# A Fourier sequence transform as seven block products in two passes, and where its coefficient sums are made

## The chip, the cores and the metric

The kernel runs on one core of one Trainium2 chip. The metric is the device time of one execution in microseconds; three runs of the kernel before are given below. The engines are TensorE (PE in the profile, its weight loads PEld), VectorE (DVE), ScalarE (ACT), GpSimd (POOL) and SyncE (SP), which issues almost all transfers of this kernel, in order.

## The reference

Four layers follow each other on x of 2048 rows and 512 columns: a Fourier mixing layer, an attention layer with a compressive memory, and both once more. Each is added to its input, which is normalised row by row first. The change concerns the Fourier layers:

```python
a = jnp.einsum("bsd,ed->bse", x, dft_hid_re)
b = jnp.einsum("bsd,ed->bse", x, dft_hid_im)
y = jnp.einsum("ts,bse->bte", dft_seq_re, a) - jnp.einsum("ts,bse->bte", dft_seq_im, b)
```

The kernel takes the sequence transform first: it multiplies the normalised rows by the real and by the imaginary sequence matrix (2048 x 2048 each), and then each result by its hidden matrix (512 x 512), summing both.

## The kernel before, in words

**Precision.** A float32 operand is used as two parts: `split` (lines 95 to 105) writes hi with a ScalarE copy (L99) and lo with a subtraction on VectorE (L101). `matmul3` (L107) makes three matmuls of them: hi by hi, hi by lo, lo by hi, each 128 x 128 by 128 x 512.

**Tiles.** The output of the sequence transform is made in four column groups (`tcn`, 0 to 3) of 512 sequence positions. The sum runs over the 2048 rows: 8 steps `k` of 128 rows in each half (`HALF` = 8), so rows `k` and `k + 8` belong together. The normalised rows are the 16 tiles `xa` (tag "w", 16 buffers), split into hi and lo. The coefficients of one `tcn` and `k` are four blocks of 128 x 512: re0, re1 (real, lower and upper half of the rows) and im0, im1.

**First transform** (`direct`). `contract` (L306) makes, for each column group, the real and the imaginary product whole: 8 k x 2 halves x 2 parts x 4 pieces of 128 columns x 3 = 384 matmuls into eight PSUM banks (tile u). `read_pairs` (L272) loads the four blocks in two transfers of 512 KB into raw buffers ("craw" for even k, half of a ring for odd k), splits them, and then forms four sums for the second transform (L296): re0+im0, im0+im1, re0+im0+im1 and re0+im0+im1+re1. They lie in the other half of the ring, one buffer of four blocks, and are stored in DRAM (`sums`, L299), 1 MiB for each `tcn` and `k`. At the end of a group ScalarE (L328) and VectorE (L330) move the eight banks to the tiles `c`.

**Second transform.** Seven products of blocks, P1 to P7, take the place of eight: per group 7 x 8 k x 2 halves x 3 = 336 matmuls (tile m, `product`, L333). Their right sides are blocks of coefficients or the stored sums; the left sides are columns of `xa`, or of `xb` and `xs`, differences and sums of rows that `add_rows` (L218) makes. For P1 and P7 the second half of the lower rows' columns has been replaced by a difference (in `normalise`, L208). `PHASES` (L52) gives the order: P1 and P7 for groups 0 and 1, P2 and P4 for these, the same for 2 and 3, then P6, P5 and P3 for all four. `read_block` (L256) loads one block for one product, 256 KB, into one of eight places of a ring (`cring`) and splits it (512 wide). `TERMS` (L43) says how a product enters the tiles `c`; VectorE adds it from PSUM (L356).

**After each sequence transform** `split_u` and `hidden` (L359 on) make the product with the hidden matrices (tile y), and the attention follows.

**Order of the work.** The kernel is written as generators, each placed on a hand-written line of slots with `place(order, generator, slots)`; a slot of the transforms is about six matmuls for one product. The program order that results is a priority: a scheduler orders each engine's instructions by it, TensorE keeps it strictly. Every `yield` is the end of one slot's part. `read_pairs` stands 12 slots ahead of its matmuls with its loads and 4 ahead with its splits; `read_block` 10 and 4 ahead. The right sides live in the tags "chi" and "clo" with three buffers each. `load_rows` (L121) uses four buffers "xt". `a1`, `b1`, `a2`, `b2` (L1002 to L1005) are the first slots of the four layers.

## Time and profile before

| | |
|---|---|
| runs of the kernel before | 1906.6, 1908.78, 1909.02 us (median 1908.78) |
| the profiled execution | 1911.1 us from its first to its last instruction (this span is the time that the profile gives for it) |
| mean granted TensorE clock | 0.985 |
| ScalarE busy | 1062.9 us, 56% |
| transfers | 296.49 MB, mean 155 GB/s |
| read from HBM, written to HBM | 192.95 MB, 100.66 MB |

How to read it: a table by stages gives, for each stretch of the span, the busy time of every engine with its number of instructions, then the granted clock (PEclk, 1.00 is full speed), the busy share of the 16 DMA engines and what they moved in GB/s. A row of the timeline gives the start, the duration, the engine, the line, the operation, out<-in and the shape; what stands in brackets is the engine's idle time before it and what ended it. A row of waits gives the sum, the number and the longest. Durations of matmuls overlap each other.

### The profile page before, as it was taken

The numbers are of one execution on the slowest core, as the hardware profiler recorded it, in microseconds if no ns is written. First come the engines' busy times: TensorE is split into PE (matmuls) and PEld (weight loads), VectorE is DVE, ScalarE is ACT, GpSimd is POOL, SyncE is SP. The second block draws the span as 40 slices with busy tenths as digits, with TensorE's granted clock in tenths as the row PEclk, the third lists the DMA queues.
The fourth block names the chain that finished last, engine by engine and source line by source line (L and its number), as shares of the span: only waits on it lengthen the run. The fifth ranks groups of instructions, "written<-read, shape, count | busy, mean of one in ns | idle before, by whom it ended". The sixth has DMA issues, their size and how long they took to land. (4 is left out here: it accounts for less than half of the span.)

```text
span 1911.1 us, 31877 instructions
## 1 busy us (share of the span) xinstructions
PE 1809.7 (95%) x10336; PEld 1301.0 (68%) x10336; DVE 1311.1 (69%) x4073; ACT 1062.9 (56%) x2292; POOL 512.5 (27%) x831
## 2 busy tenths in 40 slices
PE   7899999999899999999889999999988999999998
PEld 6678888888556656665458888787865655666654
DVE  8654545462787787777866687777558778777773
ACT  3221213331578777767664465453337877777775
POOL 4200000002345344446431000000124443434432
PEclk9999999999899999999999999999999999999998
DMA  6665555353544333434445787563444434444231
GB/s 224 233 208 199 189 191 198 115 173 121 178 125 148 118 120 115 149 119 134 134 154 181 222 251 225 164 204 127 159 150 139 144 108 134 126 133 142 91 117 45
DMA packets 165655, 296.49 MB, mean 155 GB/s; under 512 B 17776, under 2 KB 66928, under 8 KB 165488
## 3 DMA queue, kind: packets, MB, share of 16 engines
q1 hardware_dynamic: 162224, 293.68, 47.5%
q8 instruction: 81, 1.33, 0.3%
q10 hardware_dynamic: 3264, 0.79, 0.2%
q14 instruction: 86, 0.70, 0.1%
HBM read 192.95 MB, written 100.66 MB: 154 GB/s over the span
## 5 line engine op out<-in xcount | busy, mean ns | idle before, releaser
L603 DVE CUSTOM_DVE_ANT_0 junk<-nat,mask 128x512 bf16<-128x512 f32 (+3 forms) x1024 | 496.6, 485 | 203.2 <-PE nat L87 183.9
L669 ACT ACTIVATE pT<-sT 128x512 f32<-128x512 f32 x640 | 370.3, 598 | 15.0 <-ACT sT L668 2.2
L87 PE MATMUL u<-chi,xa 128*128 128x512 f32 x1024 | 321.1, 395 | 10.9 <-DVE xa L97 7.3
L672 POOL TENSOR_SCALAR_AFFINE_SELECT pT<-pT 128x256 f32<-128x256 f32 (+1 forms) x448 | 197.4, 455 | 431.5 <-ACT pT L669 366.8
L87 PE MATMUL sT<-stkq,stkk 99*128 99x256 bf16 (+3 forms) x1024 | 250.7, 307 | 17.5 <-DVE mx L603 8.8
L87 PE MATMUL nat<-stkk,stkq 96*128 96x512 bf16 (+3 forms) x1024 | 246.5, 302 | 20.8 <-DVE mx L603 12.4
L668 ACT ACTIVATE sT<-sT 128x256 f32<-128x256 f32 (+1 forms) x640 | 208.6, 334 | 63.9 <-PE sT L87 56.7
L87 PEld LDWEIGHTS u<-chi,xa 128*128 128x128 f32 x1024 | 195.4, 191 | 52.8 <-issue 7.2
L87 PE MATMUL u<-clo,xa 128*128 128x512 f32 x512 | 202.6, 396 | 9.6 <-DVE clo L101 9.6
L142 POOL TENSOR_TENSOR r<-ve,half_neg 128x2 f32<-128x2 f32 (+1 forms) x33 | 24.0, 728 | 696.5 <-DVE ve L140 692.9
L87 PE MATMUL y<-wdt,us 128*128 128x512 f32 x768 | 182.5, 391 | 1.2 <-DVE wdt L101 1.2
L87 PEld LDWEIGHTS <-stkk 99*128 99x128 bf16 x1024 | 82.6, 99 | 146.3 <-issue 127.9
L87 PEld LDWEIGHTS y<-wdt,us 128*128 128x128 f32 x768 | 143.4, 188 | 31.6 <-DVE wdt L101 2.0
L87 PE MATMUL pv_bank<-pT,vt 128*17 128x128 f32 (+3 forms) x2048 | 158.7, 440 | 1.7 <-POOL pT L672 1.6
L87 PEld LDWEIGHTS <-stkq 96*128 96x128 bf16 x1024 | 94.9, 99 | 75.9 <-issue 37.3
L87 PE MATMUL po<-wo,oh 128*128 128x512 f32 x384 | 125.7, 443 | 7.6 <-DVE oh L101 5.4
L87 PE MATMUL pvv<-wv,xT 128*128 128x512 f32 x384 | 127.0, 443 | 3.9 <-DVE mx L603 3.9
L87 PE MATMUL pqk<-xT,wq 128*128 128x512 f32 x384 | 129.9, 447 | 0.0
L87 PE MATMUL pqk<-xT,wk 128*128 128x512 f32 x384 | 127.8, 442 | 0.0
L87 PEld LDWEIGHTS u<-clo,xa 128*128 128x128 f32 x512 | 97.7, 191 | 32.5 <-DVE clo L101 12.2
L87 PEld LDWEIGHTS pv_bank<-pT,vt 128*17 128x17 f32 x2048 | 57.6, 98 | 90.7 <-issue 77.0
L99 ACT ACTIVATE clo<-cring 128x512 fp32r<-128x512 f32 x112 | 70.6, 631 | 69.1 <-DVE chi L101 37.9
(138 smaller groups left out, 3032.0 us busy)
## 6 DMA issues: line engine op xcount, KB each, us to landing
sum<-sring SPq DMA_DIRECT2D x32, 1024.0 KB
cring<-sum SPq DMA_DIRECT2D x128, 256.0 KB
stkq<-scrq SPq DMA_DIRECT2D x64, 384.0 KB
stkk<-scrk SPq DMA_DIRECT2D x64, 384.0 KB
cring<-in_ct SPq DMA_DIRECT2D x96, 256.0 KB
sring<-in_ct SPq DMA_DIRECT2D x32, 512.0 KB
xt<-mid SPq DMA_DIRECT2D x64, 256.0 KB
craw<-in_ct SPq DMA_DIRECT2D x30, 512.0 KB
```

Of the source, the lines that this page charges most:

```text
L87: return tc.keep_in_program_order(op(*args, **kwargs))
L99: A.activation(hi, src, AF.Copy, scale=scale)
L142: G.tensor_tensor(out=r, in0=ve, in1=half_neg[:, :n], op=ALU.pow)
L603: V.tensor_tensor_reduce(junk[:, :n], src, mask[:, 512 - n :], 1.0, 3e38, ALU.add, ALU.min, dst,)
L668: A.activation(blocks, blocks, AF.Relu)
L669: A.activation(dst, ps, AF.Exp, scale=-SCALE)
L672: G.affine_select(blocks, blocks, pattern=[[0, n] for n in blocks.shape[1:-1]] + [[1, P]], compare_op=ALU.is_ge, fill=0.0, base=0, channel ...
```

## The change

The first transform makes column group 0 as before. Groups 1 to 3 are made of the seven products, in two passes: P1, P2, P7 and P4 (eight PSUM banks) for each of the three groups, then P3, P5 and P6 (six banks) for each. The coefficients lie in DRAM as four blocks side by side (re1, re0, im0, im1), 8 KB per row of a partition.

- `read_direct` loads group 0 and makes no sums. Once `contract(0)` has used row tile k, `change_rows` loads its row again, normalises it and replaces the second half of `xa[k]` by the difference. `add_rows` runs during the last group of pass 1.
- `read_all` (pass 1) loads four blocks in one transfer of 1 MiB, splits P2's and P1's (1024 wide at once), makes four sums, one of them (im0+im1) on GpSimd, splits P4's and P7's, and stores two sums (512 KB).
- `read_rest` (pass 2, and the last phase of the second transform) loads the two stored sums and im1. `store_sums` makes the two sums of group 0 during pass 2.
- In the second transform `read_upper` loads three blocks and makes im0+im1 itself; `read_lower` loads one block and one stored sum, and adds them. The last phase runs in the order P3, P5, P6. Of the sums, two of four are stored.
- Raw blocks rotate over two halves of the ring, a tile "quad" (in place of "craw") and, in the first transform, the space of the attention's v tiles. In the second transform the first eight reads have the two ring halves alone.
- P6 enters one of its three terms on GpSimd, from a copy that ScalarE makes.
- The attention's tiles pT2 and praw and its v tiles lie in these shared places; the ones in the v tiles are set later. The attention and second transform start 24 slots earlier in the slot line.

```diff
-PHASES = (
-    (("P1", "P7"), (0, 1)),
-    (("P2", "P4"), (0, 1)),
-    (("P1", "P7"), (2, 3)),
-    (("P2", "P4"), (2, 3)),
-    (("P6", "P5", "P3"), range(4)),
-)
+PHASES = {
+    True: (
+        (("P1", "P2", "P7", "P4"), range(1, TC)),
+        (("P3", "P5", "P6"), range(1, TC)),
+    ),
+    False: (
+        (("P1", "P7"), (0, 1)),
+        (("P2", "P4"), (0, 1)),
+        (("P1", "P7"), (2, 3)),
+        (("P2", "P4"), (2, 3)),
+        (("P3", "P5", "P6"), range(TC)),
+    ),
+}
...
+        def raw_set():
+            if not ring:
+                ring.append(sb.tile([P, 8, 512], F32, name="cring", tag="xT", bufs=1))
+                ring.append(itertools.cycle([ring[0][:, :4], ring[0][:, 4:]]))
+                ring.append(itertools.cycle([1, 0, 0] + [2] * direct))
+            reads[0] += 1
+            if direct or 8 < reads[0]:
+                home = next(ring[2])
+                if home == 1 and reads[0] < total - 6:
+                    if len(ring) < 4:
+                        ring.append(quad("cquad"))
+                    return ring[3]
+                if home == 2:
+                    return spare[:, :4]
+            return next(ring[1])
...
+        def rights(src):
+            hi, lo = pair("chi", "chi", 3), pair("clo", "clo", 3)
+            split(hi, lo, src)
+            return [(hi[:, j], lo[:, j]) for j in range(2)]
...
+        def store_sums(tcn, k):
+            raw = raw_set()
+            nc.sync.dma_start(raw[:, 1:], ct[tcn, k, :, 1:])
+            yield
+            add(raw[:, 1], raw[:, 1], raw[:, 2])
+            add(raw[:, 3], raw[:, 1], raw[:, 3])
+            nc.sync.dma_start(sums[tcn, k], raw[:, 1::2])
+            yield
+
+        def read_all(tcn, k):
+            raw = raw_set()
+            nc.sync.dma_start(raw, ct[tcn, k])
+            yield
+            pair_sum = spare_pairs[k % 2]
+            add(pair_sum[:, 1], raw[:, 2], raw[:, 3], G)
+            right[tcn, "P2", k], right[tcn, "P1", k] = rights(raw[:, :2])
+            yield
+            add(raw[:, 2], raw[:, 1], raw[:, 2])
+            add(raw[:, 3], raw[:, 2], raw[:, 3])
+            later.append(add(pair_sum[:, 0], raw[:, 0], raw[:, 3]))
+            yield
+            right[tcn, "P4", k], right[tcn, "P7", k] = rights(pair_sum)
+            nc.sync.dma_start(sums[tcn, k], raw[:, 2:])
+            yield
+
+        def read_upper(tcn, k):
+            raw = raw_set()
+            nc.sync.dma_start(raw[:, 1:], ct[tcn, k, :, 1:])
+            yield
+            add(raw[:, 2], raw[:, 2], raw[:, 3])
+            right[tcn, "P1", k], right[tcn, "P7", k] = rights(raw[:, 1:3])
+            yield
+
+        def read_lower(tcn, k):
+            raw = raw_set()
+            nc.sync.dma_start(raw[:, 0], ct[tcn, k, :, 0])
+            nc.sync.dma_start(raw[:, 1], sums[tcn, k][:, 1])
+            yield
+            add(raw[:, 1], raw[:, 0], raw[:, 1])
+            right[tcn, "P2", k], right[tcn, "P4", k] = rights(raw[:, :2])
+            yield
+
+        def read_rest(tcn, k):
+            raw = raw_set()
+            nc.sync.dma_start(raw[:, :2], sums[tcn, k])
+            nc.sync.dma_start(raw[:, 2], ct[tcn, k, :, 3])
+            yield
+            right[tcn, "P3", k] = one_right(raw[:, 2])
+            right[tcn, "P5", k], right[tcn, "P6", k] = rights(raw[:, :2])
+            yield
...
+        def change_rows(k):
+            xt = load_rows(x_in[k])
+            yield
+            xn = normal(xt, row_mv[:, k], row_r[:, k : k + 1])
+            a, b = slice(0, D // 2), slice(D // 2, D)
+            V.tensor_tensor(out=xn[:, b], in0=xn[:, a], in1=xn[:, b], op=ALU.subtract)
+            split(xa[k][:, 0, b], xa[k][:, 1, b], xn[:, b])
             yield
...
             for m in range(2):
+                if len(TERMS[name]) > 2:
+                    copy = new_raw()
+                    A.activation(copy, ps[m], AF.Copy)
                 for j, base, op in TERMS[name]:
                     dst = c[tcn, j][:, m]
                     if base is None:
                         A.activation(dst, ps[m], AF.Copy)
+                    elif len(TERMS[name]) > 2 and j == (1, 0):
+                        G.tensor_tensor(out=dst, in0=c[tcn, base][:, m], in1=copy, op=op)
                     else:
                         V.tensor_tensor(out=dst, in0=c[tcn, base][:, m], in1=ps[m], op=op)
...
+        t = start
         if direct:
...
+            place(2, contract(0), run_from(t, 4 * HALF, 2))
+            for k in range(HALF):
+                place(3, read_direct(0, k), [t + 8 * k - 12, t + 8 * k - 4])
+                place(3, change_rows(k), [t + 8 * k + 4, t + 8 * k + 9])
+            t += 8 * HALF
+        for names, tcns in PHASES[direct]:
+            n = len(names)
+            for tcn in tcns:
+                for j, name in enumerate(names):
+                    place(2, product(tcn, name), run_from(t + j, HALF, n))
                 for k in range(HALF):
...
+                    at = {4: [-14, -7, -6, -2], 3: [-10, -5], 2: [-9, -6]}[n]
+                    place(3, readers[names](tcn, k), [t + k * n + d for d in at])
+                t += HALF * n
+        u = t - len(tcns) * 3 * HALF
+        for k in range(HALF):
+            if direct:
+                place(3, add_rows(k), [u - 25 + 4 * k, u - 24 + 4 * k])
+                place(3, store_sums(0, k), [u + 7 * k, u + 7 * k + 5])
+            else:
                 place(3, add_rows(k), [u - 48 + 6 * k, u - 44 + 6 * k])
...
-    b1 = a1 + TC * 8 * HALF + LEAD
+    b1 = a1 + (8 + 7 * (TC - 1)) * HALF + LEAD
```

More of the change, by code (lines that the diff above doesn't have):

```diff
@@ L184, in spectral_infini_kernel @@
     sums = {
-        (tcn, k): dram.tile([4, P, 512], F32, name=f"sum{tcn}_{k}") for tcn in range(TC) for k in range(HALF)
+        (tcn, k): dram.tile([P, 2, 512], F32, name=f"sum{tcn}_{k}") for tcn in range(TC) for k in range(HALF)
     }
@@ L521, in proj @@
             rem = sb.tile([P, 512], F32, name="rem", bufs=1)
[L522 removed]
+            raw = new_raw() if with_phi else rem
             sign = -1.0 if n == "q" else 1.0
```

142 lines of the change are left out of this document (66 added, 76 removed).

## The prediction

> **What bounds the kernel now.** I read the page first, then the stages of the first transform, then what TensorE waited for there, then the stages of the second transform.
>
> ```profile
> span 1911.1 us, 31877 instructions
> PE 1809.7 (95%) x10336; PEld 1301.0 (68%) x10336; DVE 1311.1 (69%) x4073; ACT 1062.9 (56%) x2292; POOL 512.5 (27%) x831
> L87 PE MATMUL u<-chi,xa 128*128 128x512 f32 x1024 | 321.1, 395 | 10.9 <-DVE xa L97 7.3
> L87 PE MATMUL u<-clo,xa 128*128 128x512 f32 x512 | 202.6, 396 | 9.6 <-DVE clo L101 9.6
> ```
>
> TensorE (PE) is busy 95% of the span. The first sequence transform is the tile u: 1024 + 512 = 1536 matmuls, 384 for each of four column groups. The duration (395 ns) overlaps the next matmul; what counts is the distance of starts. A table by stages, and two rows near the end of the transform:
>
> ```profile
> core 0: us, PE busy (x) PEld busy (x) DVE busy (x) ACT busy (x) POOL busy (x), PEclk, DMA share, GB/s
> 112.40:377.90 265.50, 265.50 (x1173) 219.84 (x1172) 134.10 (x175) 67.64 (x85) 0.00 (x0) 1.00 0.54 184
> 7.00:112.40 105.40, 91.88 (x365) 72.73 (x366) 76.33 (x147) 25.69 (x34) 32.54 (x23) 0.95 0.66 223
> ...
> 373.75 0.62 PE L87 MATMUL u<-chi,xa 128*128 128x512 f32 x2
> ...
> 377.15 0.62 PE L87 MATMUL u<-chi,xa 128*128 128x512 f32 x2
> ```
>
> Between the last two rows lie 15 matmuls in 3.40 us: 0.2267 us each. From 112.4 us on TensorE is never idle, VectorE (DVE) is half busy. All 1536 at that pace are 348.2 us; the transform took 377.9 - 7.0 = 370.9. The missing 22.7 us lie in the first group. What the engines waited for up to 150 us:
>
> ```profile
> PE u L87 <- DVE clo L101: 9.6, 6, 3.2
> PE u L87 <- ACT chi L99: 3.3, 1, 3.3
> DVE sring L296 <- DMA sum<-sring: 22.8, 5, 6.0
> ...
> 65.00:70.00 5.00, 3.51 (x17) 2.58 (x15) 5.00 (x7) 1.68 (x3) 2.65 (x3) 1.00 0.26 88
> 104.00:107.00 3.00, 0.05 (x1) 0.00 (x0) 2.84 (x4) 0.00 (x0) 0.00 (x0) 1.00 0.02 7
> 107.00:109.00 2.00, 1.75 (x5) 1.42 (x6) 2.00 (x6) 0.00 (x0) 0.00 (x0) 0.66 0.54 53
> 109.00:111.00 2.00, 2.00 (x7) 1.51 (x6) 0.89 (x3) 0.00 (x0) 0.00 (x0) 0.50 0.74 273
> ```
>
> TensorE waited 9.6 + 3.3 us for split coefficients. VectorE is late because it waits for the store of the last sums (22.8 us in all; up to 6.0 us for one 1 MiB store) before it may overwrite their single buffer. After the 3.2 us gap at 104 the granted clock is 0.66, then 0.50 for some 4 us; after the 1.5 us gap in 65 to 70 it stays 1.00. So gaps of 3 us cost more than themselves, shorter ones do not.
>
> The second transform (products P1 to P7, tile m):
>
> ```profile
> 969.60:1003.00 33.40, 31.77 (x180) 21.62 (x179) 18.16 (x35) 22.03 (x46) 10.77 (x16) 0.92 0.58 180
> 1003.00:1038.00 35.00, 35.00 (x162) 28.99 (x161) 21.33 (x39) 14.67 (x26) 3.69 (x3) 1.00 0.50 160
> 1038.00:1082.00 44.00, 44.00 (x196) 36.45 (x195) 31.66 (x55) 21.93 (x36) 3.87 (x3) 1.00 0.74 236
> 1082.00:1125.00 43.00, 43.00 (x192) 35.61 (x191) 32.62 (x59) 23.84 (x42) 0.00 (x0) 1.00 0.75 224
> 1125.00:1169.00 44.00, 44.00 (x196) 36.45 (x195) 38.98 (x73) 26.32 (x48) 0.00 (x0) 1.00 0.80 260
> 1169.00:1304.00 135.00, 133.19 (x582) 108.54 (x581) 94.77 (x156) 65.70 (x113) 0.00 (x0) 1.00 0.55 173
> ```
>
> TensorE is the bound here too; VectorE comes nearest at 1125 to 1169 (38.98 of 44), where the row sums xb and xs are made (add_rows) beside the splits of P2 and P4.
>
> **The change, part by part.** Sums are made against the span, 1911.1; the three runs' median is 1908.78, 2.3 us less, and I take the difference over to it.
>
> 1. *Matmuls.* Three groups go from 384 to 7 products x 8 k x 2 halves x 3 = 336. Removed: 144 x 0.2267 = **-32.6 us**, on the path if TensorE stays the bound. What is late next is VectorE.
>
> 2. *First group.* It loses its four sums per k and their 1 MiB store, and with them the wait of 22.8 us; the four raw buffers now rotate. It gains change_rows: a reload, one normalisation and two 256-wide operations per k. The 22.7 us lost are 12.9 of waits and some 9 at half clock. About 5 stay (first coefficients, the clock's start). Of the other 17 I take **-11**: the rows' own normalisation beside GpSimd remains. Ends: -5 to -15.
>
> 3. *Pass 1 (P1, P2, P7, P4) on VectorE.* Prices, as distances of starts where VectorE runs packed:
>
> ```profile
> 39.40 1.06 ACT L99 ACTIVATE chi<-sring 128x1024 fp32r<-128x1024 f32 x1 [1.36 <-DMA sring<-in_ct]
> ...
> 44.03 1.21 DVE L101 TENSOR_TENSOR clo<-sring,chi 128x1024 fp32r<-128x1024 f32 x1
> 45.16 1.00 DVE L159 TENSOR_SCALAR xn<-xt,row_mv,row_r 128x512 f32<-128x512 f32 x2
> ...
> 1115.83 0.55 DVE L159 TENSOR_SCALAR xn<-xt,row_mv,row_r 128x512 f32<-128x512 f32 x1
> ...
> 1119.21 0.68 DVE L101 TENSOR_TENSOR clo<-cring,clo 128x512 fp32r<-128x512 f32 x1
> 1119.81 0.68 DVE L101 TENSOR_TENSOR xb<-xn,xb 128x512 fp32r<-128x512 f32 x1
> ...
> 1121.35 0.54 DVE L159 TENSOR_SCALAR xn<-xt,row_mv,row_r 128x512 f32<-128x512 f32 x1
> ```
>
> A 1024-wide subtraction takes 45.16 - 44.03 = 1.13 after a 1.06 on ScalarE, a 512-wide one 0.60. From 1115.83 to 1121.35 stand four 512-wide splits and one add_rows: 5.52 - 2.40 = 3.1 us for an add_rows. Pass 1 needs per k two splits (2.26), three sums (1.80), an eighth of six evacuations (0.45): 4.5 us, against 24 matmuls = 5.44 us. The fourth sum is GpSimd's. Beside GpSimd VectorE is slower:
>
> ```profile
> 28.41 5.67 POOL L101 TENSOR_TENSOR xa<-xn,xa 128x512 fp32r<-128x512 f32 x2 [2.19 <-ACT xa L99]
> 32.78 1.31 POOL L101 TENSOR_TENSOR xa<-xn,xa 128x512 fp32r<-128x512 f32 x1
> 37.60 3.29 POOL L101 TENSOR_TENSOR xa<-xn,xa 128x512 fp32r<-128x512 f32 x2 [0.20 <-ACT xa L99]
> ...
> 38.37 1.27 DVE L147 TENSOR_TENSOR rt<-r 128x2 f32<-128x2 f32 x1
> 39.68 1.23 DVE L148 TENSOR_TENSOR rt<-rt,ve 128x2 f32<-128x2 f32 x1
> ...
> 49.87 0.16 DVE L148 TENSOR_TENSOR rt<-rt,ve 128x2 f32<-128x2 f32 x1
> ```
>
> In the pair at 37.60 a VectorE operation of two columns took 1.27 and 1.23 us instead of 0.16, so 1.1 us lost per GpSimd operation; in the pair at 28.41 GpSimd took the loss (2.8 us instead of 1.31). Ends 0 and 1.1, I take the middle, 0.6: 5.1 of 5.44 us, 94%. VectorE can be that full without harm to TensorE: from 1115.83 to 1121.35 it has no gap, and TensorE is busy all of 1082 to 1125. So the first two groups of pass 1 cost **+3** (0 to 8).
>
> The Trainium skill, page "SBUF — State Buffer", section "SBUF: two separate sides", says that VectorE and GpSimd share a port pair by an exclusive lock: whichever starts first has it for its whole instruction and the other is blocked, if the VectorE operation has two SBUF inputs. It speaks against giving a two-input sum to GpSimd here; by it each of them could block VectorE for all of its 1.3 us, the third case below. The pair at 37.60 agrees, and the pair at 28.41 shows the other side of it.
>
> 4. *add_rows in the third of these groups.* xb and xs take the buffers of xa, so they can only be made while the last group of pass 1 runs. A slot is six matmuls, 1.36 us. From two slots after that group's start until the fourth k of pass 2, 39 slots = 53 us, VectorE has: six first splits 6.8, six times the sums with GpSimd's share 15 (6 x 2.4), seven second splits 7.9, eight evacuations 5, seven add_rows 21.7, four reads of pass 2 at 0.60 + 1.13 = 6.9: 63 us. Loss **+11**. Ends: +6 if VectorE starts with a lead, +24 if it has none. The gaps are under 3 us each, so no clock is lost.
>
> 5. *Pass 2 (P3, P5, P6).* Per k 1.73 + ten evacuations over eight k (0.75) + store_sums of group 0 (two sums in seven slots, 0.5): 3.0 of 4.08 us. Transfers: 0.75 MiB per 4.08 us = 193 GB/s and 1.25 MiB per 9.5 us = 138: 331 GB/s for three quarters of it. Row for the most that moved:
>
> ```profile
> 45.00:50.00 5.00, 4.49 (x20) 3.38 (x18) 2.99 (x9) 1.15 (x2) 3.19 (x3) 1.00 0.98 354
> ```
>
> Just under it: **+3** (0 to 10). SyncE issues all of this in order; a store that waits for VectorE's sum holds up the loads behind it, but the loads stand five slots (6.8 us) ahead of their splits. Six-bank changeovers and the start of the hidden transform: **+1**.
>
> 6. *Second transform, VectorE.* P7 and P4 now need one sum each (0.60), splits come as one 1024-wide operation: per k 1.73 instead of 1.20. In 48 slots with add_rows: 8 x 3.1 + 24 x 1.73 + ten evacuations 6 = 72 against 65 us; now it is 60. Less a lead of 3: **+4** (0 to 8). GpSimd's part of P6: **-1**.
>
> 7. *Second transform, reads of P1 and P7.* Three blocks instead of two, in one transfer, with two buffers for the first eight reads, then three, instead of eight blocks. A load: 0.79 MB at 354 GB/s, 2.2, and about 2 us fixed (an estimate: the 1 MiB store took up to 6.0, of which 3.0 are its bytes at that pace and a part is sharing) = 4.2; then a sum 0.6, ScalarE 1.1, VectorE 1.13 and the hand-overs, 3.1: 7.3 us, so 3.65 per k with two buffers, 2.4 with three. TensorE takes 33.4 / 8 = 4.2 per k in the first group (the attention's output products run between), then 2.72. Little room: **+4** (0 to 10).
>
> At nothing: pT2, praw and the v tiles only change homes, no instruction more; six memsets of the ones columns move to an idle GpSimd.
>
> Sum: -32.6 - 11 + 3 + 11 + 3 + 1 + 4 - 1 + 4 = **-18.6 us**: 1890.
>
> **The rivals.**
> - *All hidden*: VectorE keeps a lead, the reads are in time: -32.6 - 15 + 6 + 1 = -40.6: 1868. For it: at 1125 to 1169 TensorE has no gap beside a nearly full VectorE. Against: in point 4 VectorE has more work than time.
> - *Transfers bind*: if the chip moves only 224 / 0.75 = 299 GB/s as at 1082 to 1125, pass 2 needs 331 / 299, 0.44 us more for 19 k = 8.3; a P1/P7 load takes 6.0, its round 9.1, so 3.03 instead of 2.72 for 24 k and 4.55 instead of 4.2 for 8 = 10. Instead of 3 and 4: -18.6 + 11.3 = -7: 1902. Against: rows that are longer in memory, as those at 45 to 50, moved 354.
> - *VectorE binds in pass 1*: in order, waiting for ScalarE and blocked by GpSimd, it does not run packed but, as in 7 to 112 us, is busy 76.33 of 105.40, 72%, with TensorE waiting. At 80%, between the two, the first two groups need 5.1 / 0.80 = 6.4 per k, 16 x 0.94 = 15, and point 4 gives 63 / 0.80 - 53 = 26. Instead of 3 and 11: -18.6 + 27 = +8: 1917, slower. It turns the sign from 84% down; at 72% the sum is +28. Against: outside the row normalisations there are few of the tiny operations that wait for GpSimd in 7 to 112.
> - That the matmuls do not go away cannot be: the instruction stream is fixed.
>
> **How the numbers follow.** Forecast 0.48, all hidden 0.15, transfers 0.15, VectorE 0.22 (some of which stays under 1913). The range is 1868 to 1917, from the first rival to the last; the forecast's own is 1879 to 1900. A measurement of this kernel tells 0.2% (3.8 us, so 1905 and 1913) from no change. Faster: 0.48 + 0.15 + half of transfers = 0.70; the same 0.09 (the rest of transfers and a little of VectorE); slower 0.21.
>
> **What would show it.** Matmul records 144 fewer. First group: TensorE's waits for clo down from 9.6 to under 5 us, the wait for the sums' store gone. In the last group of pass 1, VectorE over 95% busy and 8 to 14 us of TensorE idle there; none there would mean all hidden. In the other two groups under 0.2 us idle per k; 0.5 would be the VectorE rival. In pass 2 a DMA share above 0.9; waits of splits for DMA there, or in P1/P7 of the second transform, would be the transfers. Wrong altogether if gaps grow past 3 us and the clock falls.

## The result, and the profile after

The changed kernel takes **1920.13 us** (median of 13 runs, 1913.51 to 1925.84); the kernel before took 1908.78 in 13 runs beside them (1902.19 to 1914.13). The ratio is 1.0062 [1.0046, 1.0077]: slower by 0.6%, where 1890 was forecast. The profiled execution of the changed kernel is one of its longer ones; the eight kernels below that share its first transform reach the tile y 2 to 6 us earlier.

The page of the changed kernel:

```profile
span 1920.7 us, 31638 instructions
PE 1794.4 (93%) x10192; PEld 1269.8 (66%) x10192; DVE 1410.1 (73%) x4157; ACT 1096.4 (57%) x2276; POOL 565.0 (29%) x869
```

There are 10192 matmuls instead of 10336: the 144 are gone. So 32.6 us of TensorE's work were saved, and 44 us came in elsewhere. The table by stages of the changed kernel shows where; the columns are those of the prediction's tables, and the rows are group 0, the first two groups of pass 1, its third group, and pass 2 in three pieces (the tile y starts at 367.2):

```profile
7.00:113.40 106.40, 94.43 (x383) 75.73 (x384) 67.01 (x148) 32.09 (x46) 29.33 (x25) 0.97 0.59 200
113.40:205.00 91.60, 90.68 (x384) 70.68 (x383) 73.01 (x90) 35.92 (x36) 21.47 (x16) 1.00 0.71 258
205.00:255.80 50.80, 45.87 (x196) 35.94 (x196) 50.70 (x72) 22.62 (x29) 9.95 (x8) 1.00 0.73 256
255.80:290.00 34.20, 29.86 (x122) 22.68 (x121) 29.97 (x54) 16.69 (x28) 0.00 (x0) 0.97 0.79 251
290.00:330.00 40.00, 37.17 (x149) 29.18 (x148) 26.05 (x34) 14.05 (x18) 2.66 (x2) 0.94 0.83 282
330.00:367.20 37.20, 37.20 (x166) 30.79 (x165) 31.16 (x48) 20.13 (x32) 3.67 (x6) 1.00 0.74 248
```

The transform now ends at 367.2 instead of 378, 11 us earlier, not the 26 that the first six terms of the prediction add up to. Pass 1 takes 142.4 us where 576 matmuls are 130.6, pass 2 111.4 where 432 are 97.9.

The second transform, P1, P7, P2 and P4 from the first m to the first use of xs, in the changed kernel:

```profile
961.20:1035.00 73.80, 68.67 (x348) 50.92 (x347) 47.65 (x73) 33.95 (x54) 16.47 (x19) 0.98 0.61 206
1035.00:1185.00 150.00, 137.99 (x574) 105.25 (x573) 121.96 (x171) 60.03 (x69) 4.58 (x3) 1.00 0.72 231
sum 223.80, PE 206.65 PEld 156.17 DVE 169.61 ACT 93.98 POOL 21.05; mean PE 103.33 PEld 78.08 DVE 84.80 ACT 46.99 POOL 10.53
```

and the same stretch of the kernel before:

```profile
969.70:1040.00 70.30, 68.67 (x349) 52.17 (x348) 40.64 (x78) 38.24 (x73) 15.06 (x20) 0.96 0.55 174
1040.00:1172.30 132.30, 132.30 (x585) 109.61 (x584) 105.41 (x186) 71.81 (x122) 3.17 (x2) 1.00 0.75 236
sum 202.60, PE 200.97 PEld 161.78 DVE 146.05 ACT 110.05 POOL 18.23; mean PE 100.48 PEld 80.89 DVE 73.03 ACT 55.02 POOL 9.11
```

The same matmuls take 21.2 us longer (7 were forecast for the whole second transform). The last phase (P3, P5, P6) takes 130.5 us against 131.3, so nothing is lost there. What the engines waited for in the changed kernel, first TensorE in 900 to 1450 us, then VectorE and SyncE's queue (SPq) in 1035 to 1165 us:

```profile
PE m L92 <- DVE clo L106: 14.9, 18, 2.8
...
DVE cring L303 <- DMA cring<-sum: 11.8, 12, 2.7
DVE cring L303 <- DMA cring<-in_ct: 4.2, 5, 1.7
DVE cquad L303 <- DMA cquad<-sum: 3.8, 5, 1.4
...
SPq L358 <- DVE clo L106: 35.2, 17, 3.2
SPq L350 <- DVE clo L106: 33.8, 15, 4.6
```

and in the kernel before, TensorE's wait for lo and VectorE's only wait for a transfer in the same windows:

```profile
PE m L87 <- DVE clo L101: 1.8, 3, 0.6
...
DVE st L137 <- DMA xt<-mid: 1.0, 1, 1.0
```

In the changed kernel this is a ring of waits: TensorE waits for the subtraction lo, VectorE (with a sum) for a transfer, and the queue, before it may issue that transfer, for an earlier lo, which frees the place. Before, VectorE waited for no coefficients in this stretch, only once for a row. From here on a *place* is one raw buffer, a *read* is what is loaded for one k, and a *turn* is the time from one load into a place to the next load into it. One turn, in the timeline of the changed kernel (P1 and P7 of the last two groups):

```profile
1095.11 0.33 SPq L350 DMA_DIRECT2D cquad<-in_ct  x1
1104.63 0.33 SPq L350 DMA_DIRECT2D cquad<-in_ct  x1
...
1093.86 1.22 DVE L106 TENSOR_TENSOR clo<-cquad,chi 128x1024 fp32r<-128x1024 f32 x1
1101.42 0.69 DVE L303 TENSOR_TENSOR cquad<-cquad 128x512 f32<-128x512 f32 x1 [1.90 <-DMA cquad<-in_ct]
1103.37 1.23 DVE L106 TENSOR_TENSOR clo<-cquad,chi 128x1024 fp32r<-128x1024 f32 x1 [1.26 <-ACT chi L104]
...
1102.28 1.06 ACT L104 ACTIVATE chi<-cquad 128x1024 fp32r<-128x1024 f32 x1 [4.02 <-DVE cquad L303]
```

The old lo ends at 1093.86 + 1.22 = 1095.08, the load is issued at 1095.11, the sum starts 6.3 us later, then come hi and lo, and the next load is issued at 1104.63: a turn of **9.5 us**. Three places give one read in 3.17 us; the 12 matmuls of one read take 2.72. This turn is a usual one: from 1074.31 to 1122.48 us the queue loads this place six times, 9.6 us apart on average.

### The profile page after: what moved, and what is told of

It is laid out like the page before. It is cut to its first block, busy times and chain, and to the rows that moved or that the text cites. A ratio compares the mean times of both kernels' runs of the same rounds, so it can differ in the third digit from the quotient of the medians.

```text
span 1920.7 us, 31638 instructions
## 1 busy us (share of the span) xinstructions
PE 1794.4 (93%) x10192; PEld 1269.8 (66%) x10192; DVE 1410.1 (73%) x4157; ACT 1096.4 (57%) x2276; POOL 565.0 (29%) x869
## 5 line engine op out<-in xcount | busy, mean ns | idle before, releaser
L764 ACT ACTIVATE pT<-sT 128x512 f32<-128x512 f32 x640 | 370.0, 599 | 14.2 <-ACT mt L736 1.6
L92 PE MATMUL m<-chi,xa 128*128 128x512 f32 x896 | 284.1, 394 | 1.5 <-DVE c L449 1.2
L104 ACT ACTIVATE chi<-cring 128x1024 fp32r<-128x1024 f32 (+1 forms) x123 | 121.6, 989 | 152.9 <-PE m L92 69.4
L92 PE MATMUL m<-clo,xa 128*128 128x512 f32 x448 | 180.7, 403 | 20.0 <-DVE clo L106 19.6
L92 PEld LDWEIGHTS m<-chi,xa 128*128 128x128 f32 x896 | 169.0, 189 | 37.7 <-DVE c L449 2.1
L92 PE MATMUL pv_bank<-pT,v_all 128*17 128x128 f32 (+3 forms) x2048 | 158.8, 438 | 1.2 <-POOL pT L767 1.1
L106 DVE TENSOR_TENSOR clo<-cring,chi 128x1024 fp32r<-128x1024 f32 x103 | 131.4, 1276 | 37.0 <-ACT chi L104 36.5
L92 PE MATMUL m<-chi,xb 128*128 128x512 f32 x448 | 150.8, 397 | 4.9 <-ACT chi L104 3.3
L447 POOL TENSOR_TENSOR c<-c,praw 128x512 f32<-128x512 f32 x14 | 20.3, 1456 | 351.9 <-ACT praw L441 292.8
```

Source lines behind the costliest of these rows:

```text
L92: return tc.keep_in_program_order(op(*args, **kwargs))
L104: A.activation(hi, src, AF.Copy, scale=scale)
L106: lo_engine.tensor_tensor(out=lo, in0=src, in1=hi.bitcast(F32), op=ALU.subtract)
L447: G.tensor_tensor(out=dst, in0=c[tcn, base][:, m], in1=copy, op=op)
L764: A.activation(dst, ps, AF.Exp, scale=-SCALE)
```

## The experiments

Three theories stand against each other for the second transform. **A**: the turn of a place is too long for three places. **D**: VectorE runs in order, and a sum that waits for its transfer holds up the subtractions behind it. **B**: VectorE simply has too much to do. D was set up only after the first runs (e1, e2, e3, e5). In the table, "y1" is the start of the first hidden transform and "second" the time from the first m of the second transform to the first y after it, both from the profiled execution; the ratios go against the kernel before, with 95% intervals.

| kernel | y1 | second | median us | ratio |
|---|---|---|---|---|
| before | 378.1 | 333.9 | 1908.78 | |
| changed | 367.2 | 354.3 | 1920.13 | 1.0062 [1.0046, 1.0077] |
| e1_no_second_sums | 361.4 | 331.2 | 1898.10 | 0.9937 [0.9916, 0.9958] |
| e5_second_part_alone | 369.3 | 355.4 | 1925.65 | 1.0087 [1.0061, 1.0113] |
| e4_first_part_alone | 355.2 | 334.2 | 1887.81 | 0.9905 [0.9887, 0.9923] |
| e3_sums_in_group0 | 355.5 | 353.0 | 1909.77 | 1.0003 [0.9988, 1.0018] |
| e11_first_part_own_buffer | 359.5 | 333.3 | 1889.96 | 0.9904 [0.9889, 0.9918] |
| e14_first_part_no_gpsimd | 348.9 | 334.0 | 1883.03 | 0.9872 [0.9854, 0.9889] |
| e8_same_work_no_wait | 361.4 | 343.8 | 1909.73 | 1.0013 [0.9999, 1.0028] |
| e9_sums_on_gpsimd | 361.2 | 362.0 | 1923.59 | 1.0094 [1.0073, 1.0114] |
| e10_group0_and_gpsimd | 354.3 | 364.1 | 1919.19 | 1.0064 [1.0044, 1.0085] |
| e2_more_places | 361.0 | 355.4 | 1921.40 | 1.0057 [1.0037, 1.0078] |
| e12_fourth_place | 364.4 | 350.7 | 1915.24 | 1.0036 [1.0024, 1.0049] |
| e13_fourth_place_group0_own_buffer | 353.1 | 348.8 | 1904.31 | 0.9981 [0.9971, 0.9991] |
| e15_five_places | 363.9 | 353.5 | 1917.11 | 1.0050 [1.0032, 1.0068] |
| e17_five_places_gpsimd | 364.9 | 354.0 | 1919.34 | 1.0052 [1.0034, 1.0070] |
| e16_five_places_group0_no_gpsimd | 351.6 | 351.3 | 1903.08 | 0.9982 [0.9966, 0.9998] |
| e18_five_places_order | 362.7 | 338.8 | 1902.90 | 0.9975 [0.9959, 0.9991] |
| e19_all_repaired | 350.5 | 338.4 | 1886.87 | 0.9891 [0.9866, 0.9915] |

**The two halves apart.** e1 takes the two sums out of the second transform (P7 and P4 then use a block where the sum belongs):

```diff
-            add(raw[:, 2], raw[:, 2], raw[:, 3])
...
-            add(raw[:, 1], raw[:, 0], raw[:, 1])
```

> The changed kernel without the two sums that the second transform makes itself: the same transfers, but P7 gets im0 alone and P4 the stored block alone (so the result is another one). The changed kernel's second sequence transform took 354 us (before: 334), and TensorE waited for split coefficients in it. Theory A, the round of a raw place (load, sum, ScalarE, VectorE, next load) is too long for two or three places: the sum is about 1.3 us of a round of 9, so 6 to 10 us less in all, and waits of TensorE for clo remain. Theory B, the added sums simply load VectorE (64 x 0.6 us): 15 us or more less, the transform back to about 338. Theory C, the transfers bind: within 3 us of the changed kernel.

Measured: second transform 331.2 instead of 354.3, the time 22 us less. The 22 us hang on the two sums; the loads, of the same bytes into the same three places, make TensorE wait no longer without them, so the transfers alone are not the cause. It is more than the 6 to 10 us that A had allowed, and B's case.

e5 leaves the first transform at 1536 matmuls in four groups (with rotating raw buffers and two sums stored) and changes the second as the change does:

```diff
-            place(2, contract(0), run_from(t, 4 * HALF, 2))
+            for tcn in range(TC):
+                place(2, contract(tcn), run_from(t, 4 * HALF, 2))
...
+                add(raw[:, 1], raw[:, 1], raw[:, 2])
+                summed = add(raw[:, 3], raw[:, 1], raw[:, 3])
+            nc.sync.dma_start(sums[tcn, k], raw[:, 1::2])
```

> The second part of the change alone: the first transform makes all four groups as eight products, as before (1536 matmuls), but with the changed kernel's rotating raw buffers and only two sums, added in place; the second transform as in the changed kernel. If the wait for the store of the sums was what group 0 lost before, the hidden product starts at 361 to 366 us (before 378, changed 367), so the seven products gained nothing over this; the whole is 1912 to 1916, the second transform again 350 or more. Rival, group 0 is held by the row normalisation on VectorE and GpSimd: the hidden product starts at 372 or later, the whole at 1920 to 1926.

Measured: second 355.4, as in the changed kernel. The second half of the change costs its 20 us by itself. Of the first transform neither case came: y starts at 369.3, between the two, and the whole time of 1925.65 is the rival's.

e4 changes the first transform alone: it makes and stores four sums there, and the second transform loads them and adds nothing.

```diff
-        (tcn, k): dram.tile([P, 2, 512], F32, name=f"sum{tcn}_{k}") for tcn in range(TC) for k in range(HALF)
+        (tcn, k): dram.tile([P, 4, 512], F32, name=f"sum{tcn}_{k}") for tcn in range(TC) for k in range(HALF)
...
             nc.sync.dma_start(sums[tcn, k][:, :2], raw[:, 2:])
+            nc.sync.dma_start(sums[tcn, k][:, 2:], pair_sum)
```

> The first part of the change alone: seven products in two passes in the first transform, but all four sums stored (group 0's from the blocks it loads anyway), and the second transform reads them as before and makes none itself. Pass 1 then moves 2 MiB in 5.44 us, 385 GB/s. If that binds at 354: pass 1 takes 10 to 13 us longer than 142, the hidden product starts at 364 to 370; if not, at 354 to 358. The second transform without sums: 331 to 335 by theories B and D. Whole 1886 to 1900, so faster than before; above 1905 if the second transform is late for another reason than its sums.

Measured: 1887.81, 1% faster than before. Pass 1 moves 343 GB/s in its first two groups (258 in the changed kernel) and takes 142.6 us, no more than the changed kernel: that transfers would bind there was a miss. Seven products in the first transform gain; the gain was then paid out again in the second.

**The first transform.** e3 makes group 0's two sums from the blocks that group 0 loads anyway, in place of store_sums:

```diff
+            with behind_first(k == 0):
+                add(raw[:, 1], raw[:, 1], raw[:, 2])
+                add(raw[:, 3], raw[:, 1], raw[:, 3])
+            nc.sync.dma_start(sums[tcn, k], raw[:, 1::2])
...
-                place(3, store_sums(0, k), [u + 7 * k, u + 7 * k + 5])
```

> The changed kernel with the two sums of column group 0 made from the blocks that group 0 loads anyway, and stored then, instead of being loaded again during pass 2. In the changed kernel pass 2 took 111.6 us where its 432 matmuls need 97.9. If the transfers of these sums make pass 2 late: pass 2 at 100 to 103 us, in all 8 to 10 us faster, group 0 at most 3 us slower. Rival, pass 2 is late for its own reads and its evacuations: pass 2 stays above 108 and the whole within 3 us.

Measured: 10.4 us less than the changed kernel, pass 2 99.8 us instead of 111.4. What ScalarE waited for in 256 to 362 us of the changed kernel, and then the middle of pass 2 in e3:

```profile
ACT chi L104 <- DMA cring<-sum: 6.8, 3, 4.4
ACT chi L104 <- DMA cquad<-sum: 5.7, 1, 5.7
```

```profile
290.00:330.00 40.00, 40.00 (x178) 33.14 (x177) 28.87 (x37) 20.67 (x30) 5.69 (x4) 1.00 0.51 169
```

store_sums (768 KB in, 512 KB out per k) made pass 2's loads late: the DMA share is 0.83 with it and 0.51 without, and TensorE is then not idle in this stretch. e3 moves the sums' VectorE work out of pass 2 as well, but VectorE was not the bound there (26.05 us of 40). What held the loads up, the rate, the places that store_sums takes from the rotation or the queue's order, is not told apart.

e11 is e4 with the row of change_rows in a buffer of its own (`praw`) instead of one of the two xn buffers. It also overwrites one sum of pass 1 that waits in `praw` (P7, group 1, k = 1).

```diff
-            xn = normal(xt, row_mv[:, k], row_r[:, k : k + 1])
+            xn = praw[:, k % 2]
+            V.tensor_scalar(
+                xn, xt, row_mv[:, k, 0:1], row_r[:, k : k + 1], op0=ALU.subtract, op1=ALU.mult
+            )
```

> The first part alone (four sums made in the first transform and stored, none in the second), and change_rows normalises into the space praw, which nothing else uses then, instead of one of the two xn buffers that it shares with normalise. If sharing is what holds VectorE up in group 0 (it waited for GpSimd to finish with xn, 4.4 us, and TensorE waited 10.8 us for clo up to 113): the first group gets 3 to 6 us shorter, the hidden transform starts at 349 to 352 instead of 355.2, and the time is 1882 to 1885. Rival: the reload and the work itself hold it up, wherever the row goes: no change, 1887 to 1889.

Measured: no gain (group 0 ends at 116.0 instead of 111.2). VectorE's wait for xn that the trace of e4 shows is gone, and the first group is not shorter: my reading of that wait was wrong.

e14 is e4 with pass 1's fourth sum on VectorE:

```diff
-            add(pair_sum[:, 1], raw[:, 2], raw[:, 3], G)
+            add(pair_sum[:, 1], raw[:, 2], raw[:, 3])
```

> The first part alone, with the sum im0+im1 of pass 1 on VectorE instead of GpSimd; nothing else. My prediction took 0.6 us per k off VectorE for GpSimd's share of the port, and GpSimd's sum is also awaited by the other sums (11 us of VectorE's time in 111 to 205 us). If that is what pass 1 loses (142.6 us instead of 130.6): VectorE gains 11 and pays 24 x 0.6 = 14 for the sums, so it comes out nearly even: pass 1 takes 140 to 144 us, 1886 to 1890. If VectorE's work is the bound by itself: pass 1 4 to 10 us longer, 1892 to 1898. If GpSimd's blocking costs more than its waits show: pass 1 134 to 139, 1880 to 1885.

Measured: 1883.03, the **fastest of all**, 4.8 us less than e4; pass 1 takes 138.2 us instead of 142.6, the third case. ScalarE's copies to c mark the end of each group of pass 1, first in the changed kernel, then in e14:

```profile
154.74 1.06 ACT L445 ACTIVATE c<-m 128x512 f32<-128x512 f32 x2
201.03 1.06 ACT L445 ACTIVATE c<-m 128x512 f32<-128x512 f32 x2
252.71 1.06 ACT L445 ACTIVATE c<-m 128x512 f32<-128x512 f32 x2
```

```profile
150.27 1.07 ACT L444 ACTIVATE c<-m 128x512 f32<-128x512 f32 x2
194.35 1.06 ACT L444 ACTIVATE c<-m 128x512 f32<-128x512 f32 x2
```

and the row of 160 to 208 us in e14's table by stages:

```profile
160.00:208.00 48.00, 46.62 (x204) 37.51 (x203) 44.33 (x57) 19.82 (x21) 0.00 (x0) 1.00 0.92 341
```

A group of 192 matmuls is 43.5 us at full pace. With GpSimd's sum the second group takes 46.29 (45.60 in e4), without it 44.08, although VectorE is then busy 44.33 of 48 us: 92% full harms little, and GpSimd's sum cost more than it took over. Part of that is waiting for its result: VectorE waited 11.4 us for GpSimd in 111 to 205 us of e4, and not at all in e14. How much is blocking is not told apart.

**The second transform: what it is not.** e8 keeps the sums' work but adds data that is always there (P7 and P4 use a block in place of the sum):

```diff
-            add(raw[:, 2], raw[:, 2], raw[:, 3])
+            add(praw[:, 0], praw[:, 1], praw[:, 1])
...
-            add(raw[:, 1], raw[:, 0], raw[:, 1])
+            add(praw[:, 0], praw[:, 1], praw[:, 1])
```

> The changed kernel with each of the second transform's two sums replaced by a VectorE addition of the same size on a tile that is long there (so P7 and P4 get other data, and the result is another one). VectorE has the same work as in the changed kernel, but does not wait for a transfer in it. The kernel without these sums had its second transform in 331 us, the changed kernel in 354. Theory B, the added work loads VectorE: second transform 348 to 354, whole 1914 to 1920. Theory D, VectorE works in order and a sum that waits for its transfer holds up the splits behind it: second transform 332 to 340, whole 1898 to 1906.

Measured: second 343.8, between the two cases, and inconclusive: the scheduler put 55 of the 64 sums into 900 to 1035 us, the end of the attention and the first reads, and the other nine before. In 1035 to 1165 us TensorE was busy throughout, but none of the added work stood there.

e9 puts the two sums on GpSimd, e10 adds e3 to it:

```diff
-            add(raw[:, 1], raw[:, 0], raw[:, 1])
+            add(raw[:, 1], raw[:, 0], raw[:, 1], G)
```

> The changed kernel with the second transform's two sums on GpSimd, which is idle there: now GpSimd waits for the transfer. The sum takes 1.3 us instead of 0.6, so a round of a raw place is longer. Theories B and D both expect most of the 23 us back: second transform 333 to 342, whole 1900 to 1908; if the round of a place were what counts (theory A), it is slower than the changed kernel, 1922 or more. If GpSimd's lock on VectorE costs 0.6 us each (64 of them), some 10 us of the gain stay away: 345.

> Group 0's sums from its own blocks together with the second transform's sums on GpSimd. If the two gains add up: 1909.8 less 12 to 18, so 1892 to 1898, faster than the kernel before by 0.6% or more. If GpSimd's lock takes the gain: 1904 to 1910.

Measured: slower still, 362 and 364. For e9 that is A's case (1922 or more); for e10 both cases missed. I first read this as VectorE's load refuted (B); e17 below shows that GpSimd's sums slow VectorE itself, so these two runs don't separate the theories.

**More places.** e2 gave three-block reads four places and two-block reads six, and issued the loads earlier:

```diff
+                if n == 3:
+                    sets = [(q[:, 0:2], q[:, 2:3]), (r[:, 0:2], r[:, 2:3]), (r[:, 3:5], r[:, 5:6]), (r[:, 6:8], q[:, 3:4])]
+                else:
+                    sets = [(q[:, 0:2],), (r[:, 0:2],), (r[:, 2:4],), (r[:, 4:6],), (q[:, 2:4],), (r[:, 6:8],)]
```

> The changed kernel with the same work, but raw places of the size that a read needs: from the ninth read on, four places for three blocks and six for two (instead of three of four blocks for all), and loads issued some slots earlier. Theory A (the round of a place): 8 to 14 us faster, the second transform near 342, waits of TensorE for clo in P2 and P4 nearly gone. Theory B (VectorE's work): within 3 us. Theory C (transfer rate): within 3 us.

Measured: no gain (355.4). At the changes of stage its places overlap, so some blocks are overwritten before they are split; nothing is rested on it alone.

e12 adds one place, in the space of the attention's v tiles, from the 21st read on:

```diff
+        four = [itertools.cycle([1, 0, 2, 0])]
...
-                home = next(ring[2])
+                home = next(ring[2] if direct or reads[0] <= 20 else four[0])
```

> The changed kernel with one more place for raw blocks in the second transform: from the 21st read on, places rotate over the quad, the two ring halves and the space of the attention's v tiles (not read between 991 and 1400 us), four instead of three; the ones of the v tiles are set once more afterwards. Sums, transfers and VectorE's work stay. Theory A (a place's round is too long): 9.5 us over four places are 2.4 per k, less than the 2.72 that the matmuls take, so TensorE's waits for clo in 1035 to 1165 us (9.6 us in the changed kernel) fall under 2, the second transform (first m to first y) takes 337 to 344 instead of 354, and the time is 10 to 14 us less than the changed kernel's 1920: 1906 to 1910. Theory D (VectorE runs in order, and a sum that waits for its transfer holds up the subtractions behind it, however many places there are): the waits stay, the second transform takes 352 to 356, 1918 to 1922.

> The changed kernel, whole, with three of its losses taken away: the sums of group 0 made from the blocks that group 0 loads anyway (measured alone: pass 2 shorter by 11 us, 1909.8), a fourth place in the second transform (10 to 14 by theory A, 0 by theory D), and change_rows in a buffer of its own (3 to 6, or 0). By theory A with the buffer's gain: 1890 to 1897. By theory D and without it: 1908 to 1911.

Measured: second 350.7 in e12, 3.6 us less than the changed kernel, between the two theories and nearer D; TensorE still waited 9.1 us in 1035 to 1165. e13 (e12 with e3 and e11's edit, and so with e11's overwritten sum) gave 348.8 and 1904.31, again the middle: 1890 to 1897 was expected by A, 1908 to 1911 by D.

e15 has five places of three blocks, e17 the same with the sums on GpSimd, e16 is e15 with e3's and e14's edits:

```diff
+            if not direct and 20 < reads[0]:
+                if not homes:
+                    r, q = ring[0], ring[3]
+                    of = [spare[:, :3], spare[:, 3:], q[:, :3], r[:, :3], r[:, 3:6]]
+                    homes.append(itertools.cycle(enumerate(of)))
```

> The changed kernel with five places of three blocks in the second transform from the 21st read on (two in the space of the v tiles, one in the quad, two in the ring) instead of three; sums, transfers and VectorE's work stay. If the round of a place is the cause, with one place taken up by the sum that VectorE runs ahead: with four places three were in effect turning, with five four are, 9.5 us / 4 = 2.4 per k against 2.72: TensorE's waits in 1035 to 1165 us (9.6 us in the changed kernel, 9.1 with four places) fall under 2, first m to first y takes 336 to 342, 1904 to 1908 us. If VectorE's order or the amount of transfers is the cause: waits of 7 to 9 us, 348 to 352, 1914 to 1917.

> As the kernel with five places, and the two coefficient sums of the second transform on GpSimd. VectorE then waits for no transfer. With three places this was the slowest (first m to first y 362). If the number of places is the cause, GpSimd's longer sum (1.3 to 2.8 us instead of 0.69) is covered by five places: 336 to 344, 1904 to 1910. If VectorE's order is the cause and not the places: also 336 to 344, but then the kernel with five places and VectorE's sums is 8 to 14 us behind it. If the transfers are the cause: over 348 in both.

> The changed kernel with its losses taken away together: group 0's sums from the blocks that group 0 loads (11 us, as measured), pass 1's fourth sum on VectorE (5 us, as measured with the first part alone), five places in the second transform (12 to 16 if the round of a place is the cause, 4 if not). If the three add up and the round is the cause: 1886 to 1893, within a few us of the first part alone with the fourth sum on VectorE (1883). If the round is not the cause: 1898 to 1902.

Measured: 353.5, 354.0 and 351.3. Two places more change next to nothing: **A alone falls**. By what was expected, over 348 in both e15 and e17 stood for the transfers; e1 (the same bytes) and e18 below rule them out. The timeline of e15 shows what held it up:

```profile
1076.22 2.35 DVE L106 TENSOR_TENSOR clo<-cring,chi 128x1024 fp32r<-128x1024 f32 x2
1079.02 0.69 DVE L312 TENSOR_TENSOR cquad<-cquad 128x512 f32<-128x512 f32 x1 [0.44 <-DMA cquad<-in_ct]
1082.07 0.69 DVE L312 TENSOR_TENSOR cring<-cring 128x512 f32<-128x512 f32 x1 [2.35 <-DMA cring<-in_ct]
1082.68 1.22 DVE L106 TENSOR_TENSOR clo<-v_all,chi 128x1024 fp32r<-128x1024 f32 x1
...
1077.59 1.06 ACT L104 ACTIVATE chi<-v_all 128x1024 fp32r<-128x1024 f32 x1 [2.03 <-PE m L92]
...
1083.95 0.50 PE L92 MATMUL m<-clo,xa 128*128 128x512 f32 x1 [0.71 <-DVE clo L106]
```

The hi of a read was done at 1077.59 + 1.06 = 1078.65, but its lo ran at 1082.68: two sums of later reads stood ahead of it, the second waited 2.35 us for its transfer, and TensorE waited for the lo. Here the order shows, not the number of places.

In e17 VectorE waits for no coefficients (once, 1.3 us, for a row), but GpSimd's sums run beside it. VectorE's operations on 256 columns in the timeline of e17:

```profile
1144.80 0.41 DVE L251 TENSOR_TENSOR xn<-xn 128x256 f32<-128x256 f32 x1
1145.25 1.40 DVE L252 TENSOR_TENSOR xn<-xn 128x256 f32<-128x256 f32 x1
```

and the row of 1035 to 1165 us in e17, above that of the changed kernel:

```profile
1035.00:1165.00 130.00, 119.19 (x513) 94.97 (x512) 103.02 (x111) 52.45 (x62) 75.20 (x46) 1.00 0.76 247
```

```profile
1035.00:1165.00 130.00, 119.99 (x500) 91.58 (x499) 103.01 (x142) 51.07 (x57) 4.58 (x3) 1.00 0.71 231
```

A 0.41 us operation takes 1.40, and VectorE without the sums is as busy (103.02) as the changed kernel's with them (103.01). The Trainium skill, page "SBUF — State Buffer", section "SBUF: two separate sides", describes an exclusive lock on the ports that the two engines share; e17 agrees with it. That this alone made e17 late is not shown: GpSimd itself waited 49.7 us for transfers in this stretch, with its later sums behind.

**The order.** e18 is e15 with each sum issued behind the lo of the second read before it (`made` holds the lo instructions):

```diff
+        def behind_second_last():
+            return nullcontext() if reads[0] <= 20 else tc.issue_after(made[-2].ins)
...
-            add(raw[:, 1], raw[:, 0], raw[:, 1])
+            with behind_second_last():
+                add(raw[:, 1], raw[:, 0], raw[:, 1])
```

> The kernel with five places, and each of VectorE's sums in the second transform from the 21st read on is issued behind the subtraction (lo) of the second read before it; nothing else. In the kernel with five places sums ran up to three reads ahead, and VectorE waited 23.5 us for transfers in 1035 to 1165 us. If VectorE's order is the rest of the cause: these waits fall under 5 us, TensorE's under 3, first m to first y takes 336 to 344 instead of 353.5, and the time is 8 to 15 us less than with five places alone: 1902 to 1909. If it is not (VectorE's total work, or the transfers): 350 to 356, 1914 to 1919.

Measured: second 338.8 instead of 353.5, the time 1902.90, 14.2 us less than e15: as the order's theory expected. The row of 1035 to 1165 us and a piece of the timeline of e18:

```profile
1035.00:1165.00 130.00, 128.73 (x567) 105.67 (x566) 117.81 (x168) 59.81 (x69) 3.85 (x2) 1.00 0.82 268
```

```profile
1062.91 0.69 DVE L317 TENSOR_TENSOR v_all<-v_all 128x512 f32<-128x512 f32 x1
1064.33 1.23 DVE L106 TENSOR_TENSOR clo<-cring,chi 128x1024 fp32r<-128x1024 f32 x1 [0.73 <-ACT chi L104]
1065.47 0.69 DVE L317 TENSOR_TENSOR v_all<-v_all 128x512 f32<-128x512 f32 x1
1067.05 1.23 DVE L106 TENSOR_TENSOR clo<-v_all,chi 128x1024 fp32r<-128x1024 f32 x1 [0.89 <-ACT chi L104]
```

Sum and lo alternate every 2.72 us, TensorE's pace. In the whole stretch VectorE waits mostly for ScalarE's hi (10.0 us) and never for a transfer. VectorE is busy 117.81 of 130 us, more than in any kernel above, and TensorE 128.73: that refutes B, and at 268 GB/s the transfers are no bound either. Of the 4.9 us that are left against the kernel before, most lie ahead of 1029 us (TensorE 68.33 of 73.6), where the first 20 reads still use two or three places and the old order.

The same order with only the three places wasn't tried. In 1035 to 1185 us of the changed kernel no sum stands ahead of the lo of the second read before it anyway, but some stand ahead of the lo of the read just before: the sum at 1077.92 waited 2.71 us for its transfer, and the lo behind it, whose hi was done at 1076.43, began at 1078.53. So the order costs something with three places too. That places alone bring at most 3.6 us (e12, e15) and that places and order together bring 15.5 (e18) is shown; that the order alone would not, since three turns of 9.5 us give 3.17 us for each read, is worked out, not shown.

e19 puts all the repairs together (e3, e14's edit, e18):

> The same order in the kernel that also makes group 0's sums from its own blocks and pass 1's fourth sum on VectorE (1903.1 without the order). If the order is the rest of the cause: 1888 to 1895. If not: 1900 to 1904.

Measured: 1886.87, a little under the first case. The changed kernel loses 33.3 us to it; the parts measured singly, 10.4 (e3), 4.8 (e14 against e4) and 17.2 (e18), make 32.4.

## Why the prediction was wrong, step by step

1. *Matmuls, -32.6*: held. The page counts 144 fewer, and e14, in which little waiting is left in the first transform, reaches y at 348.9 instead of 378.1.
2. *First group, -11*: -3 (383 matmul records by 113.40 against 365 by 112.40; the other kernels with this first transform end the group at 111.4 to 113.5). The wait for the sums' store is gone as forecast, but TensorE's wait for clo is not:

```profile
PE u L92 <- DVE clo L106: 10.8, 4, 4.0
```

   The rotating buffers alone were worth nearly what I said: e5, which has no change_rows, shows in the same stretch

```profile
7.00:113.00 106.00, 97.01 (x406) 78.36 (x407) 69.51 (x135) 29.72 (x39) 29.20 (x23) 0.98 0.58 201
```

   406 records, about 9 us ahead of the kernel before. I had counted change_rows inside the -11 without a price of its own. By what it holds up the group stays open; the xn buffers are not it (e11).
3. *Pass 1, first two groups, +3*: +4.5 (91.6 us against 87.1 for 384 matmuls), 2.8 of it in the second group. What I took for GpSimd's sum, 0.6 for each k, was too low: without that sum (e14) the second group loses 0.6 us in all, though VectorE has more to do.
4. *add_rows, +11*: the third group took 50.8 us from its first to its last matmul, +7.3 (51.68 and +8.2 by the copies to c), with VectorE busy 50.70 of 50.80 and TensorE 45.87: there VectorE binds, as forecast, for a little less. The sum as written gives 10, not 11 (63 less 53).
5. *Pass 2, +3, and changeovers and the hidden transform's start, +1*: +13.5, and +8 to +11 in the eight kernels that share this pass (106 to 109 us). The term that failed is store_sums, whose VectorE work I priced but whose transfers I only added to a mean rate: that "the loads stand five slots (6.8 us) ahead of their splits" did not hold: the load behind the longest wait was issued at 278.58, its split began at 285.45, and ScalarE stood idle 5.67 us for it (e3 has none of these waits).
6. and 7. *Second transform, +4 -1 +4*: +20.4. This is the step that turned the sign. I priced a load at 4.2 us and a turn at 7.3, so 2.4 per k with three places; the load took 6.3 and the turn 9.5, 3.17 per k. The rival "transfers bind" had almost these sizes (6.0, 9.1, 3.03), by luck: its 6.0 has no working (0.79 MB at its 299 GB/s and 2 us are 4.6), and the rate was no bound (268 GB/s in e18). It had them only for P1 and P7: for P2 and P4, which have the same three places and the same sum ahead of the split, I priced VectorE's time (step 6) and not the turn. And I didn't see that a sum ahead of its split puts a transfer's wait into VectorE's own order, which, once there are places enough, is most of the loss (14.7 of 19.6 us over the kernel before, e15 and e18).

Together -32.6 - 3 + 4.5 + 7.3 + 13.5 + 20.4 = +10; the two profiled executions differ by 9.6.

Of the rivals, "VectorE binds in pass 1" had the sign and nearly the size (1917) for a cause that didn't act: pass 1 came out 2 us better than forecast. The range missed by 3 us; that P2/P4, store_sums' transfers and change_rows would each cost was outside of all cases.

## What to carry to other kernels

A step that is put between a load and the work that frees its buffer lengthens that buffer's turn: compare the whole turn (issue, landing, every engine's step, the next issue) divided by the number of buffers with the bound engine's time for one, for every stage that uses the buffers. An engine that runs in order hands a transfer's wait to everything behind the instruction that waits; here more buffers did not mend that (e15), an order did (e18). Work that takes no time on the bound engine can still make it wait by its transfers, which share the queue, the buffers and the rate with the loads that it needs.

## What the runs showed of the hardware

**The clock falls after shorter gaps than I had said.** In pass 2 of the changed kernel, TensorE's gaps in the timeline, and then two rows of the table by stages:

```profile
286.56 0.50 PE L92 MATMUL m<-chi,xb 128*128 128x512 f32 x1 [2.20 <-ACT chi L104]
287.82 0.61 PE L92 MATMUL m<-clo,xb 128*128 128x512 f32 x1 [0.76 <-DVE clo L106]
...
320.91 0.50 PE L92 MATMUL m<-chi,xb 128*128 128x512 f32 x1 [1.08 <-ACT chi L104]
322.17 0.80 PE L92 MATMUL m<-clo,xb 128*128 128x512 f32 x1 [0.76 <-DVE clo L106]
```

```profile
288.00:290.00 2.00, 2.00 (x6) 1.51 (x7) 2.00 (x4) 0.63 (x1) 0.00 (x0) 0.52 0.56 172
...
323.00:324.00 1.00, 1.00 (x3) 0.76 (x3) 0.85 (x1) 0.39 (x1) 0.00 (x0) 0.50 0.75 238
```

After gaps of 2.20 and 0.76 us, with one matmul between them in the timeline, the granted clock was 0.52, and after two of 1.08 and 0.76 us it was 0.50. The Trainium skill, page "TensorE: Matmul & The Clock Gate", section "Part 1: The HAM clock gate", names an idle window of about 3.4 us for this; the first pair of gaps spans 3.5 us with its matmul, but the second only 2.3 (319.8 to 322.2), which is shorter, and the measurement decides. My sentence that gaps under 3 us cost no clock was wrong for gaps close together.

**A sum on GpSimd** cost more than the middle I took: a VectorE operation of 0.41 us beside it took 1 us longer (e17), and the second group of pass 1, with eight GpSimd sums, took 1.5 us longer than without them (45.60 in e4 against 44.08 in e14), waits for their results included.
